# An attention and MLP backward kernel on one core: six late weight-gradient stores moved to the last two heads, the last MLP piece moved by four heads, and the first K load moved ahead of wq and wo

## The chip, the cores and the metric

The kernel runs on one core of a Trainium2 chip. Time is device microseconds of one execution. Three timed runs of the kernel before gave a median of 756.13 us (755.35 to 757.45). Smaller is better.

The core has a matrix engine (TensorE, PE), VectorE (DVE), ScalarE (ACT), GpSimd (POOL) and SyncE (SP). Each works through its own instructions in order. Sixteen DMA engines move data between device memory and the on-chip buffers. SP issues all large loads (queue q1 of the profile) and POOL issues all stores of gradients (queue q0).

## What is computed

One token is decoded through an attention block and a gated MLP in parallel, and the gradients of everything but one unused copy of x are taken back.

```python
xn  = layernorm(x)                       # 1 x 640
q   = xn @ wq                            # 32 heads of 128
p   = softmax(q . k_cache * 128**-0.5)   # per head, 8192 positions
o   = p . v_cache
h   = silu(xn @ w1) * (xn @ w3)          # 1728 wide
out = x + o @ wo + h @ w2
# returned: out, and the gradients for grad_out of
# x, k_cache, v_cache, wq, wo, w1, w3, w2
```

All arrays are bfloat16. k_cache and v_cache are 32 x 8192 x 128, 2 MB per head each. Their gradients are as large, and each is an outer product: dV of a head is p times do (the gradient of o), dK is ds times q. So the kernel reads some 152 MB and writes 151 MB, nearly all of it K, V, dK and dV.

## The kernel before

The loop goes over heads, with h from -1 to 31. An iteration finishes head h (called c in the code) and prepares head h + 1 (called n), and VectorE's order is the order in which the code is written. In one iteration VectorE does four products of a 2 MB tile half with a broadcast vector (`product`, line 270: two halves for the scores S of head n with K, two for DP with V), whose sums TensorE takes by multiplying with an identity (line 272), and four output tiles (`outer`, line 279: two halves of dV, two of dK of head c). Of a dV half, 24 of 32 position columns are made by VectorE and eight by ScalarE (line 283). Each output tile is one store of 1 MB, issued by POOL (line 285), from a pool of five buffers.

K and V have three buffers each. In iteration h the loads of V and K of head h + 3 are put into SP's queue (lines 113 and 107), each as soon as the code has used the buffer of head h. SP issues in order, so a load that waits for its buffer holds all later loads.

wq and wo are taken in groups of four heads (`load_group`, lines 119 to 125), two buffers each. Group g + 1 is loaded at the end of the iteration with h = 4g and prepared (`prep_steps`: q and do of four heads) in the following two. After the last head of a group, `finish_group` writes the gradients over the weights' own buffers and POOL stores them (line 238 for wo, line 242 for wq).

The MLP is cut into four pieces of 432 of its 1728 columns. A piece has one buffer `wt`, shared by all pieces, which holds w1, w3 and w2 of the piece (lines 146 to 150). The table `mlp_at` (line 462) says after which head a piece is loaded: 1, 9, 17 and 21 for pieces 0 to 3. Two heads later its steps are queued. `gap()` runs one step, four or five times a head, and steps of `prep_steps` and of the MLP wait in one list. A piece needs six steps, the first with VectorE's product at line 374, the last with the sum at line 452. So pieces 0 to 3 begin in heads 3, 11, 19 and 23 and end one head later. Its gradients are written over its weights and stored by POOL at line 431 and 433 (w2), and 446 (w1, then w3).

Before the loop, SP loads x, then wq and wo of group 0, then K and V of heads 0, 1 and 2 (lines 153 to 156). q of group 0 needs wq, do needs wo.

`row_dots` (line 321 to 325) takes the sum over DP times p. Its multiply writes a scratch tile `junk` that nothing reads. `E` holds a head's exponentials, and ScalarE reads it at line 311 for its share of dV.

After the loop, out and the gradient of x are formed from sums that were kept in `accbank` (lines 516 to 539).

The functions that the change touches, and the loop that calls them:

Of the kernel before, what the change touches and what calls it, by code (L numbers as in the profile page):

```python
# [10 lines left out]
F32 = mybir.dt.float32  # L11
ALU = mybir.AluOpType
ACTF = mybir.ActivationFunctionType
# [3 lines left out]
P = 128  # L17
# [4 lines left out]
def kernel(  # L22
# [22 lines left out]
    nc = tc.nc  # L45
    H = A_k_cache.shape[1]
    SK = A_k_cache.shape[2]
    DH = A_k_cache.shape[3]
# [4 lines left out]
    J = SK // P  # L53
    JH = J // 2
    RUN = 8
    GH = 4
    NG = H // GH
    ORDERED = {mybir.EngineType.DVE, mybir.EngineType.SP, mybir.EngineType.Pool}
    NPIECE = 4
    ACT_J = 8  # L60
    scale = float(DH) ** -0.5
# [8 lines left out]
    small = ctx.enter_context(tc.tile_pool(name="small", bufs=2))  # L70
# [7 lines left out]
    dkc = out_2.rearrange("b h (p j) d -> (b h) p j d", p=P)  # L78
    dvc = out_3.rearrange("b h (p j) d -> (b h) p j d", p=P)
    wq_v = A_wq.rearrange("(ci p) n -> p ci n", p=P)  # L80
    wo_v = A_wo.rearrange("(h p) c -> p h c", p=P)
    dwq_v = out_4.rearrange("(ci p) n -> p ci n", p=P)
    dwo_v = out_5.rearrange("(h p) c -> p h c", p=P)
# [5 lines left out]
    with tc.manual_schedule(engines=ORDERED):  # L89
# [15 lines left out]
        def load_k(h):  # L105
            Kt = kvpool.tile([P, J, DH], BF16, name="Kt", tag="K")
            nc.sync.dma_start(Kt[:], kc[h])
            kv_tiles[h] = kv_tiles.get(h, [None, None])
            kv_tiles[h][0] = Kt

        def load_v(h):
            Vt = kvpool.tile([P, J, DH], BF16, name="Vt", tag="V")
            nc.sync.dma_start(Vt[:], vc[h])
            kv_tiles[h] = kv_tiles.get(h, [None, None])
            kv_tiles[h][1] = Vt

        grp = {}

        def load_group(g):
            hs = slice(g * GH * DH, (g + 1) * GH * DH)  # L120
            wq_g = wload.tile([P, NC, GH * DH], BF16, name="wq_g", tag="wq_g")
            nc.sync.dma_start(wq_g[:], wq_v[:, :, hs])
            wo_g = wload.tile([P, GH, D], BF16, name="wo_g", tag="wo_g")
            nc.sync.dma_start(wo_g[:], wo_v[:, g * GH:(g + 1) * GH, :])
            grp[g] = dict(wq=wq_g, wo=wo_g)

        assert F % NPIECE == 0
        FP = F // NPIECE
# [9 lines left out]
        def load_piece(pc):  # L138
# [11 lines left out]
                nc.sync.dma_start(w2c[0:FP - NF * P, NF, :], B_w2[f0 + NF * P:f0 + FP, :])  # L150
            ml[pc] = (w1c, w3c, w2c)

        load_group(0)
        for h in range(min(3, H)):
            load_k(h)
            load_v(h)

# [77 lines left out]

        def finish_group(g):
            G_ = grp.pop(g)
            nc.gpsimd.dma_start(dwo_v[:, g * GH:(g + 1) * GH, :], G_["wo"][:])
            for ci in range(NC):
                nc.scalar.activation(G_["wq"][:, ci, :], G_["dqbc"][:].rearrange("p h d -> p (h d)"),  # L240
                                     ACTF.Copy, scale=xn_col[:, ci:ci + 1])
            nc.gpsimd.dma_start(dwq_v[:, :, g * GH * DH:(g + 1) * GH * DH], G_["wq"][:])


        hs = {}
# [26 lines left out]
                nc.tensor.matmul(ps[:], lhsT=ident_bf[:], rhs=T[:, :, RUN * i:RUN * (i + 1)],  # L272
                                 start=(half == 0 and i == 0), stop=(half == 1 and i == DHH // RUN - 1))

        def outer(st, vec, w2, dst, h, half, wf=None):
            j0 = half * JH
            JD = JH - (ACT_J if wf is not None else 0)
            ot = opool.tile([P, JH, DH // 2, 2], BF16, name="ot", tag="o")
            nc.vector.tensor_tensor(ot[:, 0:JD],  # L279
                                    vec.rearrange("p (a b) -> p a b", b=2).unsqueeze(1).to_broadcast([P, JD, DH // 2, 2]),  # L280
                                    w2[:, j0:j0 + JD, :].unsqueeze(2).to_broadcast([P, JD, DH // 2, 2]), ALU.mult)
            for j in range(JD, JH):
                nc.scalar.activation(ot[:, j].rearrange("p a b -> p (a b)"), vec, ACTF.Copy,  # L283
                                     scale=wf[:, half, j - JD:j - JD + 1])
            nc.gpsimd.dma_start(dst[h][:, j0:j0 + JH, :], ot[:].rearrange("p j a b -> p j (a b)"))  # L285
# [17 lines left out]
        def probs(st):  # L303
            rZ = small.tile([P, 1], F32, name="rZ")
            nc.vector.reciprocal(rZ[:], st.hb[:, 3:4])
            st.P2 = small.tile([P, J, 2], BF16, name="P2")
            nc.vector.tensor_scalar(st.P2[:], st.E[:].unsqueeze(2).to_broadcast([P, J, 2]), rZ[:], None, ALU.mult)
            st.Pf = None
            if ACT_J:
                st.Pf = small.tile([P, 2, ACT_J], F32, name="Pf")  # L310
                nc.scalar.activation(st.Pf[:], st.E[:].rearrange("p (a j) -> p a j", a=2)[:, :, JH - ACT_J:JH],
                                     ACTF.Copy, scale=rZ[:])

        def attend(st):
            for j in range(J):
# [3 lines left out]
        def row_dots(st):  # L319
            st.DP = small.tile([P, J], F32, name="DP_sb")  # L320
            nc.vector.tensor_reduce(st.DP[:], st.ps["DP"][:], AX.X, ALU.add)  # L321
            junk = small.tile([P, J], F32, name="junk", bufs=1)
            rdot = small.tile([P, 1], F32, name="rdot")
            nc.vector.scalar_tensor_tensor(junk[:], st.DP[:], 1.0, st.P2[:, :, 0], ALU.mult, ALU.mult, accum_out=rdot[:])
            nc.tensor.matmul(st.hb[:, 4:5], lhsT=ones_f[:], rhs=rdot[:], start=True, stop=True, skip_group_check=True)

        def dscores(st):
# [36 lines left out]
        def mlp_steps(pc):  # L364
# [63 lines left out]
                nc.scalar.copy(bc_sb[:, wi, :], bc_ps[:, 0:FP])  # L428
            for bi, (b0, rows) in enumerate(pblocks):
                nc.scalar.activation(w2c[0:rows, bi, :], g_bc_bf[0:rows, :], ACTF.Copy, scale=hcol[0:rows, bi:bi + 1])  # L430
            nc.gpsimd.dma_start(out_8[f0:f0 + NF * P, :].rearrange("(fb p) c -> p fb c", p=P), w2c[:, 0:NF, :])
            if NB > NF:
                nc.gpsimd.dma_start(out_8[f0 + NF * P:f0 + FP, :], w2c[0:FP - NF * P, NF, :])
            dx_ps = ps_w.tile([P, NC, DR1], F32, name="dx_ps", tag="w")
            for wi, (wt, dst) in enumerate(((w1c, dw1_v), (w3c, dw3_v))):
                yield
                T = tpool.tile([P, NC, FP], BF16, name="T13", tag="T")
                nc.vector.tensor_tensor(T[:], wt, bc_sb[:, wi, :].unsqueeze(1).to_broadcast([P, NC, FP]), ALU.mult)
                for i in range(FP // DR1):
                    nc.tensor.matmul(dx_ps[:], lhsT=ident_bf[:], rhs=T[:, :, DR1 * i:DR1 * (i + 1)],  # L440
                                     start=(wi == 0 and i == 0), stop=(wi == 1 and i == FP // DR1 - 1))
                nc.vector.tensor_tensor(wt.rearrange("p c (a b) -> p c a b", b=2),
                                        bc_sb[:, wi, :].rearrange("p (a b) -> p a b", b=2).unsqueeze(1)
                                        .to_broadcast([P, NC, FP // 2, 2]),
                                        xn2[:].unsqueeze(2).to_broadcast([P, NC, FP // 2, 2]), ALU.mult)
                nc.gpsimd.dma_start(dst[:, :, f0:f0 + FP], wt)
            yield
            if pc == 0:
                nc.vector.tensor_reduce(dxn_mlp[:], dx_ps[:], AX.X, ALU.add)
# [9 lines left out]
            if steps and next(steps[0], "end") == "end":  # L459
                steps.pop(0)  # L460

        mlp_at = {h0: pc for pc, h0 in enumerate((1, 9, 17, 21))}
        for _ in prep_steps(0):
            pass
        for h in range(-1, H):
            n = new_head(h + 1) if h + 1 < H else None
            c = hs.pop(h) if h >= 0 else None
            if h >= 0:
                g, hh = divmod(h, GH)
                if h - 2 in mlp_at:  # L470
                    steps.append(mlp_steps(mlp_at[h - 2]))
            if n:
                product(n, "S", 0)
            if c:
                probs(c)
                outer(c, c.do, c.P2, dvc, h, 0, c.Pf)
                gap()
                row_dots(c)
                attend(c)
            if n:  # L480
                product(n, "S", 1)
            if c:
                outer(c, c.do, c.P2, dvc, h, 1, c.Pf)
                if h + 3 < H:
                    load_v(h + 3)
                gap()
                dscores(c)
                outer(c, c.q, c.U2, dkc, h, 0)
            if n:
                row_max(n)  # L490
                product(n, "DP", 0)
            if c:
                outer(c, c.q, c.U2, dkc, h, 1)
                if h + 3 < H:
                    load_k(h + 3)
                gap()
            if n:
                exps(n)
                product(n, "DP", 1)
            if c:  # L500
                weights(c)
                gap()
                if hh == 0 and g + 1 < NG:
                    load_group(g + 1)
                if hh == 1 and g + 1 < NG:
                    steps.append(prep_steps(g + 1))
                    gap()
                if hh == 2 and g + 1 < NG:
                    gap()
                if h in mlp_at:  # L510
                    load_piece(mlp_at[h])
# [58 lines left out]
```

## Time and profile before

| What | Value |
|---|---|
| Median of three runs | 756.13 us |
| Profiled execution's own time | 755.72 us |
| Its span on the core | 753.9 us |
| TensorE clock granted, mean | 0.768 of full speed |
| Moved between memory and buffers | 304 MB, 403 GB/s over the span |
| Output stores | 128 of 1 MB, median 14.7 us from issue to landing |
| K loads, V loads | 32 each of 2 MB, median 16.7 and 14.2 us |
| wq and wo loads | 8 each of 640 KB, median 19.4 and 25.8 us |
| Loads of a piece: w1 and w3, w2 | 540 KB each, 480 + 60 KB; median 35.6, 33.3 and 15.6 us |

The profile is of one execution. Its rows of engines by time slice cut the span into 40 equal parts, and a digit is the busy share of a slice in tenths (9 is 90% or more). In a row of a group of instructions stand the line, engine, operation and tiles, then how many, busy time, mean duration, and the engine's idle time in front of them with what ended most of it. In a row of the timeline stand the start and the duration in us, and in brackets how long the engine sat idle in front of it and what it waited for. In a table of stretches stand the stretch, its length, then the busy time and number of instructions of TensorE, its weight loads, VectorE, ScalarE and GpSimd, then TensorE's clock, the DMA share and GB/s. SPq and POOLq are the sequencers that issue DMAs.

### The profile page before, as it was taken

The page shows a single profiled execution, that of the slowest core. Times are in us where ns is not written, and L with a number is a line of the kernel's source. Part 1 is how long each engine was busy: PE and PEld are TensorE (multiplying, and loading weights), DVE is VectorE, ACT ScalarE, POOL GpSimd, SP SyncE. Part 2 cuts the span into 40 slices and gives each one's busy share as a digit, 9 for nine tenths or more (in the row PEclk, how much of TensorE's full clock was granted, in tenths as well). Part 3 has the DMA queues.
Part 4 walks back from the last instruction along what each step waited for, and adds up shares of the span by engine and source line. Part 5 has one row for each costly group of instructions (what it writes and reads, how often), then busy time and mean ns, then how long its engine had stood idle before and what let it go on. Part 6 is the DMA issues. An engine that isn't in the chain of part 4 may idle for free.

```text
span 753.9 us, 15362 instructions
## 1 busy us (share of the span) xinstructions
PE 555.0 (74%) x6451; PEld 325.0 (43%) x6451; DVE 669.8 (89%) x732; ACT 310.1 (41%) x866; POOL 97.9 (13%) x172
## 2 busy tenths in 40 slices
PE   3787677878776678786877667867868788777672
PEld 2354344445443445443544344434534545434342
DVE  4899879999997679999999868899969999999894
ACT  4334417235443542533435144343542534443244
POOL 0011012011110101200011100121101211011011
PEclk9869967579976785878979687587966677987675
DMA  8999999999999999999999999999999999999857
GB/s 324 425 425 420 415 418 407 388 421 429 426 424 421 421 417 419 362 398 427 426 425 419 420 419 420 409 348 417 427 411 428 369 406 428 429 424 425 372 224 293
DMA packets 50201, 304.00 MB, mean 403 GB/s; under 512 B 5460, under 2 KB 21780, under 8 KB 25556
## 3 DMA queue, kind: packets, MB, share of 16 engines
q1 hardware_dynamic: 26612, 151.51, 49.1%
q0 software_dynamic: 22720, 151.35, 48.9%
q8 instruction: 50, 0.82, 0.4%
q10 hardware_dynamic: 800, 0.17, 0.1%
q14 instruction: 19, 0.16, 0.1%
HBM read 151.67 MB, written 151.34 MB: 402 GB/s over the span
## 4 chain that ended last, share of the span: by engine, by line
DVE 37%; DMA 35%; SPq 11%; PE 8%; issue 7%; POOL 1%; POOLq 0%; DVEq 0%
DMA out_dram<-ot 18%; DVE T L270 16%; DVE ot L279 12%; DMA wt<-in_B_w_dram 11%; SPq L148 6%; DMA wo_g<-in_A_wo_dram 4%; SPq L147 3%; PE psS L272 2%; PE psDP L272 2%; DMA Kt<-in_A_k_cache_dram 2%; DVE DP_sb L321 1%; DVE S_sb L289 1%; PE hb L332 1%; PE dh_ps L377 1%; PE hb L316 1%
## 5 line engine op out<-in xcount | busy, mean ns | idle before, releaser
L272 PE MATMUL psDP<-T,ident_bf 128*128 128x512 bf16 x512 | 187.7, 531 | 76.1 <-DVE T L270 76.1
L272 PEld LDWEIGHTS <-ident_bf 128*128 128x128 bf16 x1024 | 121.4, 121 | 233.6 <-issue 181.6
L283 ACT ACTIVATE ot<-do_g,Pf 128x128 bf16<-128x128 bf16 x512 | 155.7, 392 | 14.2 <-DMA out_dram<-ot 13.7
L270 DVE TENSOR_TENSOR T<-Kt,qs_g 128x4096 bf16<-128x4096 bf16 x64 | 146.4, 2289 | 9.5 <-PE psDP L272 6.3
L272 PE MATMUL psS<-T,ident_bf 128*128 128x512 bf16 x512 | 150.6, 444 | 5.6 <-DVE T L270 5.4
L279 DVE TENSOR_TENSOR ot<-qs_g,U 128x4096 bf16<-128x4096 bf16 x64 | 146.4, 2288 | 4.3 <-DMA out_dram<-ot 3.4
L270 DVE TENSOR_TENSOR T<-Vt,do_g 128x4096 bf16<-128x4096 bf16 x64 | 146.0, 2281 | 0.0
L285 POOL DMA_DIRECT2D out_dram<-ot x128 | 68.8, 538 | 577.6 <-ACT ot L283 278.3
L279 DVE TENSOR_TENSOR ot<-do_g,P 128x3072 bf16<-128x3072 bf16 x64 | 112.3, 1755 | 10.0 <-DMA out_dram<-ot 8.8
L300 ACT ACTIVATE E<-S_sb,negM 128x64 f32<-128x64 f32 x32 | 11.1, 347 | 190.9 <-DVE negM L297 190.9
L332 PEld LDWEIGHTS <-Kt 128*128 128x128 bf16 x2048 | 58.5, 99 | 21.5 <-issue 18.7
L332 PE MATMUL hb<-U,Kt 128*128 128x1 bf16 x2048 | 57.5, 164 | 7.4 <-DVE U L329 7.1
L316 PEld LDWEIGHTS <-Vt 128*128 128x128 bf16 x2048 | 57.4, 99 | 0.0
L316 PE MATMUL hb<-P,Vt 128*128 128x1 bf16 x2048 | 56.4, 163 | 0.0
L346 ACT ACTIVATE wo_g<-g_bc_bf,odq 128x640 bf16<-128x640 bf16 x32 | 26.5, 827 | 70.2 <-PE accbank L344 70.1
L292 PE MATMUL hb<-ident_f,mrow 128*128 128x128 f32 x64 | 17.7, 365 | 26.4 <-DVE mrow L291 26.4
L356 ACT ACTIVATE dq_diag<-ident_bf,odq 128x128 bf16<-128x128 bf16 x32 | 12.9, 402 | 52.8 <-DVE odq L340 52.8
L351 ACT COPY wqT<-ps_wqT 128x640 bf16<-128x640 bf16 x32 | 21.7, 680 | 15.3 <-PE ps_wqT L349 15.3
L225 ACT COPY woT<-ps_t 128x512 bf16<-128x512 bf16 x40 | 22.3, 581 | 13.4 <-PE ps_t L223 13.4
L430 ACT ACTIVATE wt<-g_bc_bf,hcol 128x640 bf16<-128x640 bf16 (+1 forms) x16 | 12.4, 821 | 36.9 <-DVE t L410 18.7
L223 PE MATMUL ps_t<-ident_bf,wo_g 128*128 128x128 bf16 x160 | 17.8, 244 | 10.6 <-DMA wo_g<-in_A_wo_dram 10.5
L301 PEld LDWEIGHTS hb<-rsum,ones_f 128*128 128x128 f32 x64 | 16.3, 271 | 21.1 <-ACT E L300 19.3
(122 smaller groups left out, 479.7 us busy)
## 6 DMA issues: line engine op xcount, KB each, us to landing
out_dram<-ot POOLq DMA_DIRECT2D x128, 1024.0 KB, 14.7
Kt<-in_A_k_cache_dram SPq DMA_DIRECT2D x32, 2048.0 KB, 16.7
Vt<-in_A_v_cache_dram SPq DMA_DIRECT2D x32, 2048.0 KB, 14.2
wq_g<-in_A_wq_dram SPq DMA_DIRECT2D x8, 640.0 KB, 19.4
wo_g<-in_A_wo_dram SPq DMA_DIRECT2D x8, 640.0 KB, 25.8
out_dram<-wo_g POOLq DMA_DIRECT2D x8, 640.0 KB, 7.3
out_dram<-wq_g POOLq DMA_DIRECT2D x8, 640.0 KB, 5.9
wt<-in_B_w_dram SPq DMA_DIRECT2D x8, 540.0 KB, 35.6
```

Of the source, the lines that this page charges most:

```text
L147: nc.sync.dma_start(w1c, w1_v[:, :, f0:f0 + FP])
L148: nc.sync.dma_start(w3c, w3_v[:, :, f0:f0 + FP])
L225: nc.scalar.copy(woT[:], ps_t[:])
L270: nc.vector.tensor_tensor(T[:], src[:, :, ds_], vec[:, ds_].unsqueeze(1).to_broadcast([P, J, DHH]), ALU.mult)
L272: nc.tensor.matmul(ps[:], lhsT=ident_bf[:], rhs=T[:, :, RUN * i:RUN * (i + 1)], start=(half == 0 and i == 0), stop=(half == 1 and i == DHH ...
L279: nc.vector.tensor_tensor(ot[:, 0:JD], vec.rearrange("p (a b) -> p a b", b=2).unsqueeze(1).to_broadcast([P, JD, DH // 2, 2]), w2[:, j0:j0 ...
L283: nc.scalar.activation(ot[:, j].rearrange("p a b -> p (a b)"), vec, ACTF.Copy, scale=wf[:, half, j - JD:j - JD + 1])
L285: nc.gpsimd.dma_start(dst[h][:, j0:j0 + JH, :], ot[:].rearrange("p j a b -> p j (a b)"))
L316: nc.tensor.matmul(st.hb[:, 0:1], lhsT=st.V[:, j, :], rhs=st.P2[:, j, 0:1], start=(j == 0), stop=(j == J - 1), skip_group_check=True)
L332: nc.tensor.matmul(st.hb[:, 1:2], lhsT=st.K[:, j, :], rhs=st.U2[:, j, 0:1], start=(j == 0), stop=(j == J - 1), skip_group_check=True)
L346: nc.scalar.activation(G_["wo"][:, hh, :], g_bc_bf[:], ACTF.Copy, scale=odq[:, 0:1])
L351: nc.scalar.copy(wqT[:], ps_wqT[:])
```

## The change

Three things change in what the kernel issues, and one in what it writes.

- The start table has 25 in place of 21 for the last MLP piece: its loads follow those of head 28, its steps run in heads 27 and 28.
- Six stores are collected in a list and issued at the top of the iteration with h = 30, ahead of everything else in it: the four of the last MLP piece (w2 in two parts, w1, w3) and the two of the next to last weight group (wo and wq of group 6). All other stores stay where they are.
- K of head 0 is loaded ahead of wq and wo of group 0, V of head 0 behind them.
- `row_dots` writes its scratch result over `E` of the same head in place of `junk`.

The rest of the difference moves an argument of `outer` to another place and drops a condition that is always true.

```diff
         grp = {}
+        late = []
+
+        def store(dst, src, later=False):
+            if later:
+                late.append((dst, src))
+            else:
+                nc.gpsimd.dma_start(dst, src)
...
+        load_k(0)
         load_group(0)
-        for h in range(min(3, H)):
+        load_v(0)
+        for h in range(1, min(3, H)):
             load_k(h)
             load_v(h)
...
         def finish_group(g):
             G_ = grp.pop(g)
-            nc.gpsimd.dma_start(dwo_v[:, g * GH:(g + 1) * GH, :], G_["wo"][:])
+            store(dwo_v[:, g * GH:(g + 1) * GH, :], G_["wo"][:], g == NG - 2)
...
-            nc.gpsimd.dma_start(dwq_v[:, :, g * GH * DH:(g + 1) * GH * DH], G_["wq"][:])
+            store(dwq_v[:, :, g * GH * DH:(g + 1) * GH * DH], G_["wq"][:], g == NG - 2)
...
-            junk = small.tile([P, J], F32, name="junk", bufs=1)
             rdot = small.tile([P, 1], F32, name="rdot")
-            nc.vector.scalar_tensor_tensor(junk[:], st.DP[:], 1.0, st.P2[:, :, 0], ALU.mult, ALU.mult, accum_out=rdot[:])
+            nc.vector.scalar_tensor_tensor(st.E[:], st.DP[:], 1.0, st.P2[:, :, 0], ALU.mult, ALU.mult, accum_out=rdot[:])
...
-            nc.gpsimd.dma_start(out_8[f0:f0 + NF * P, :].rearrange("(fb p) c -> p fb c", p=P), w2c[:, 0:NF, :])
+            last_pc = pc == NPIECE - 1
+            store(out_8[f0:f0 + NF * P, :].rearrange("(fb p) c -> p fb c", p=P), w2c[:, 0:NF, :], last_pc)
             if NB > NF:
-                nc.gpsimd.dma_start(out_8[f0 + NF * P:f0 + FP, :], w2c[0:FP - NF * P, NF, :])
+                store(out_8[f0 + NF * P:f0 + FP, :], w2c[0:FP - NF * P, NF, :], last_pc)
...
-                nc.gpsimd.dma_start(dst[:, :, f0:f0 + FP], wt)
+                store(dst[:, :, f0:f0 + FP], wt, last_pc)
...
-        mlp_at = {h0: pc for pc, h0 in enumerate((1, 9, 17, 21))}
+        mlp_at = {h0: pc for pc, h0 in enumerate((1, 9, 17, 25))}
...
                 if h - 2 in mlp_at:
                     steps.append(mlp_steps(mlp_at[h - 2]))
+            if h == H - 2:
+                for dst, src in late:
+                    store(dst, src)
             if n:
                 product(n, "S", 0)
```

More of the change, by code (lines that the diff above doesn't have):

```diff
@@ L273, in product, with outer @@
                                  start=(half == 0 and i == 0), stop=(half == 1 and i == DHH // RUN - 1))
-        def outer(st, vec, w2, dst, h, half, wf=None):
+        def outer(st, vec, w2, wf, dst, h, half):
             j0 = half * JH
@@ L307, in probs @@
             nc.vector.tensor_scalar(st.P2[:], st.E[:].unsqueeze(2).to_broadcast([P, J, 2]), rZ[:], None, ALU.mult)
[L308 to L312, printed above, removed]
+            st.Pf = small.tile([P, 2, ACT_J], F32, name="Pf")
+            nc.scalar.activation(st.Pf[:], st.E[:].rearrange("p (a j) -> p a j", a=2)[:, :, JH - ACT_J:JH],
+                                 ACTF.Copy, scale=rZ[:])
         def attend(st):
@@ L475 @@
                 probs(c)
-                outer(c, c.do, c.P2, dvc, h, 0, c.Pf)
+                outer(c, c.do, c.P2, c.Pf, dvc, h, 0)
                 gap()
@@ L482 @@
             if c:
-                outer(c, c.do, c.P2, dvc, h, 1, c.Pf)
+                outer(c, c.do, c.P2, c.Pf, dvc, h, 1)
                 if h + 3 < H:
@@ L487 @@
                 dscores(c)
-                outer(c, c.q, c.U2, dkc, h, 0)
+                outer(c, c.q, c.U2, None, dkc, h, 0)
             if n:
@@ L492 @@
             if c:
-                outer(c, c.q, c.U2, dkc, h, 1)
+                outer(c, c.q, c.U2, None, dkc, h, 1)
                 if h + 3 < H:
```

## The prediction

> **What bounds the kernel now.** I read the page's busy shares and slices, then the queues, then VectorE's waits, then a table of stretches cut at the four places where VectorE takes up an MLP piece (line 374), and last VectorE's timeline there and at the end.
>
> ```profile
> PE 555.0 (74%) x6451; PEld 325.0 (43%) x6451; DVE 669.8 (89%) x732; ACT 310.1 (41%) x866; POOL 97.9 (13%) x172
> DVE  4899879999997679999999868899969999999894
> DMA  8999999999999999999999999999999999999857
> q1 hardware_dynamic: 26612, 151.51, 49.1%
> q0 software_dynamic: 22720, 151.35, 48.9%
> ```
>
> Two resources are nearly full: VectorE at 89%, and the DMA engines, whose two queues take 98% of the span between them and whose row is 9 until three slices from the end. So a gain must come out of transfer time that ends late, and only as long as VectorE is not last.
>
> ```profile
> 98.00:281.00 183.00, 138.50 (x1613) 81.37 (x1613) 165.52 (x176) 74.95 (x211) 24.17 (x41) 0.76 1.01 418
> 281.00:465.00 184.00, 137.48 (x1619) 81.09 (x1617) 166.01 (x177) 76.37 (x216) 23.84 (x41) 0.78 1.01 413
> 465.00:562.00 97.00, 75.20 (x858) 43.85 (x856) 87.84 (x101) 41.74 (x118) 14.28 (x24) 0.75 1.00 402
> 562.00:699.00 137.00, 107.83 (x1261) 63.05 (x1259) 129.59 (x142) 55.69 (x155) 19.25 (x32) 0.76 1.01 416
> 712.00:734.00 22.00, 17.30 (x206) 10.15 (x205) 21.58 (x23) 9.53 (x31) 2.14 (x4) 0.77 0.57 232
> 734.00:754.00 20.00, 5.41 (x146) 4.62 (x144) 9.43 (x21) 9.14 (x22) 3.76 (x6) 0.60 0.71 276
> ```
>
> The third pair of numbers is VectorE's busy time, the last two are the DMA share and GB/s. Up to 562 the DMA share is 1.00 and VectorE idles 9 to 18 us in each stretch. From 562 on VectorE idles little (7.4 of 137 us), and from 712 to 734 it is full while DMA is at 0.57.
>
> ```profile
> DVE T L374 <- DMA wt<-in_B_w_dram: 18.7, 4, 6.0
> DVE U L329 <- PE hb L316: 13.6, 5, 5.5
> DVE ot L279 <- DMA out_dram<-ot: 12.3, 10, 3.1
> ```
>
> VectorE's idle time in the loop is waiting for weights (directly, and through TensorE's in-order queue at line 316) and for a free output buffer.
>
> ```profile
> 97.78 1.49 DVE L374 TENSOR_TENSOR T<-wt,g_bc_bf 128x2560 bf16<-128x2560 bf16 x1 [5.85 <-DMA wt<-in_B_w_dram]
> 280.87 1.49 DVE L374 TENSOR_TENSOR T<-wt,g_bc_bf 128x2560 bf16<-128x2560 bf16 x1 [3.64 <-DMA wt<-in_B_w_dram]
> 464.73 1.49 DVE L374 TENSOR_TENSOR T<-wt,g_bc_bf 128x2560 bf16<-128x2560 bf16 x1 [3.17 <-DMA wt<-in_B_w_dram]
> 553.91 1.76 DVE L279 TENSOR_TENSOR ot<-do_g,P 128x3072 bf16<-128x3072 bf16 x1
> 561.69 1.49 DVE L374 TENSOR_TENSOR T<-wt,g_bc_bf 128x2560 bf16<-128x2560 bf16 x1 [6.02 <-DMA wt<-in_B_w_dram]
> 699.42 1.76 DVE L279 TENSOR_TENSOR ot<-do_g,P 128x3072 bf16<-128x3072 bf16 x1 [3.10 <-DMA out_dram<-ot]
> 714.84 1.76 DVE L279 TENSOR_TENSOR ot<-do_g,P 128x3072 bf16<-128x3072 bf16 x1
> 732.35 1.76 DVE L279 TENSOR_TENSOR ot<-do_g,P 128x3072 bf16<-128x3072 bf16 x1
> ```
>
> These rows carry the sum. Pieces 0 to 3 begin at 97.78, 280.87, 464.73 and 561.69 (heads 3, 11, 19, 23), each after a wait for its weights. The last row is the first dV product of head 31; it ends at 734.11, and 19.8 us later the span ends.
>
> That the stretches are transfer-bound can be worked out. From the trace's packets, spread over 16 engines: a K or V load takes 4.99 us, an output store 2.50, a group's wq and wo 3.7 in and 3.4 out, a piece's weights 4.8 in and 5.1 out. Eight heads with two groups and a piece: 16 x 4.99 + 32 x 2.50 + 2 x 7.1 + 9.9 = 183.9, against 183.1 and 183.9 measured between pieces. Four heads with one group and a piece: 96.9, against 97.0. A piece thus begins when the transfers ahead of it are done.
>
> **The change, part by part.**
> *Piece 3 moves by four heads* (the start heads go from 21 to 25). Its loads go behind K of head 28 in SP's queue, its steps from heads 23 and 24 to 27 and 28. The stretch from piece 2 to piece 3 becomes heads 19 to 27 with groups at 20 and 24: the same transfers as in the two eight-head stretches. I take their mean, 183.5: piece 3 starts at 464.7 + 183.5 = 648.2. In the trace of before the same place in head 27 is passed at 652.4; it arrives 4 us earlier, but with the piece's VectorE work still to do.
>
> What comes after it: after piece 2 VectorE ran from 464.73 to 555.67, four heads and the piece in 90.9 us, 1.4 of it idle, though transfers were at 1.00. The same work follows piece 3 now, less the S product that head 31 has no successor for (732.35 - 714.84 = 17.5 against a usual 19.75: 2.2). So the first dV product of head 31 ends at 648.2 + 90.9 - 2.2 = 736.9, against 734.1: **+2.8 us**. As a check by idle time from 464.73 to there: before, 1.4 + 6.0 + 1.3 + 4.7 (four waits for output buffers at 657 to 702) = 13.4. After, an eight-head stretch has 15.2 (1.2 + 2.0 + 3.3 + 5.5 + 3.2) and the rest 1.4: 16.6, or +3.2.
>
> *Stores held back.* Six stores leave the queue of POOL in heads 27 and 28 (w2 in two parts, wo, wq, w1, w3; 5.1 + 3.4 = 8.5 us of engine time) and stand in front of head 30's. Nothing waits for their buffers: no later piece or group takes them. They free transfer time between 648 and 715, where the forecast has VectorE as the bound already: worth 0. The cover is VectorE's 90.9 us. Without it, at most the 4.7 us of output-buffer waits were to be had, and I have counted those as gone. Above, those waits could stay, +4.7. I take none, by the nearest row: the stretch after piece 2 had none with its stores in place.
>
> In POOL's queue they cost 0.78 + 0.53 + 0.78 + 0.88 + 0.87 + 0.87 = 4.7 us, between head 29's last issue (709.8) and head 30's first (718.4): a gap of 8.1, so it fits. Their data runs from about 713 + 3. From 715 to 741 the store queue was busy 14.0 of 26 us, so 12 are free for 8.5: 0, and at most 8.5 if all of it came ahead of the last stores. The end of the kernel (last four output stores, wo and wq of group 7, DMA share 0.71) stays 19.8 us.
>
> *K of head 0 first.* In the trace wq landed at 8.1, wo at 9.9, K at 14.8, and the first product began at 14.9. Now K takes the front (5.0 us), wq lands about 12.5, and TensorE's five products with the copy (10.73 to 13.68: 2.95) end about 15.5: VectorE starts 0.6 later. Bounds: wq right behind K at 11.6 gives -0.3, wq as last of the three at 14.8 gives +2.9. V of head 0 keeps its place. wo, needed for the V product at 22.2, is 5.1 us from do_g and comes at about 20. Price 0 either way: VectorE waits 5.85 at piece 0, more than any of these, and the DMA engines never run dry (1.02 from 5 to 98). Without that cover, +0.6.
>
> *The scratch of row_dots becomes E.* VectorE's multiply now waits until ScalarE has read E (line 311). That reading ended before the multiply in all 32 heads, by 0.27 us or more. Cost 0; half a microsecond of delay in the nine tightest heads would be some 2 us, inside the transfer-bound stretches.
>
> Sum: +2.8 on a span of 753.9, 756.7. The profiled execution took 755.72 (1.8 outside the span), 0.4 under the median of 756.13; the forecast for the median is 758.9.
>
> One rule speaks against the held-back run of issues. The Trainium skill (SBUF — State Buffer, "SBUF: two separate sides") says that VectorE in its two-port mode locks GpSimd out of the SBUF port that it writes DMA descriptors through, so that such DMAs look blocked. Here it would make each of six issues wait for an operation of 2.28 us; this trace doesn't show it: POOL issued at 590.27 and 591.14, 0.88 and 0.87 us each, beside VectorE's products.
>
> **The rivals.**
> *Weights in time* (faster). If piece 3 didn't have to wait, 5.5 + 3.2 of the 15.2 idle would go: piece 3 at 639.5, 5.9 under before, 750.2. For it: SP has nothing else to fetch between groups. Against: all four pieces waited, and the transfers add up to the stretch. It decides where piece 3 starts before 645.4. Chance 0.12, with all 8.5 us coming off the end (747.6) in it.
> *Half of that* (no change). Only the wait at line 374 goes: 2.8 - 3.2, 755.7. Chance 0.12.
> *Output buffers still late* (slower). The waits of 4.7 us return in heads 28 to 30, because loads of four more tiles and stores compete until about 700: 763.6. Chance 0.08.
> *A stretched run of issues* (slower). POOL held at each issue: 6 x 2.28 = 13.7 in place of 4.7, so head 30's first store is issued at 727 and its buffer, which head 31 wants at 737.8, is free at about 740: some 3 us more, 762. Chance 0.02. The end of 8.5 us (all the held-back data ahead of the last stores, 767) has less than 0.01 and stays outside the range.
>
> **How the numbers follow.** The forecast holds 0.66, from 757 to 760.5 (mostly the 183.1 to 183.9 of the stretch and +-1 in its place). About 0.3% (2.3 us) is what a measurement of this kernel can tell from no change; 0.72 of the forecast's chance lies above that. Slower: 0.66 x 0.72 + 0.10 = 0.58. Same: 0.18 + 0.12 = 0.30. Faster: 0.12. The range reaches down to half the wait gone, 755.0, and up into the output-buffer case, 762.5.
>
> **What would show it.** Piece 3's line-374 product near 648 after a wait for weights of 3 us or more; a DMA share of 1.00 until about 700; VectorE with under 2 us idle from there to head 31; six issues at about 713 to 718 and a DMA share near 0.9 from 715 to 725; an unchanged 19.8 us at the end; the first product at about 15.5. I am wrong if piece 3 starts before 645, if the wait there is gone, or if waits for output buffers stay in heads 28 to 30.

## The result and the profile after

The changed kernel takes 760.01 us (median of six runs, 758.98 to 761.36), the kernel before 756.01 (six runs, 755.35 to 757.45). The ratio is 1.0046, 95% interval 1.0031 to 1.0062: slower by 0.46%, some 3.5 us (the two medians lie 4.0 apart, the profiled spans 3.3). Forecast were 758.9 us and +2.8. The profiled execution took 758.98 us, with a span of 757.2; the one of before took 755.72 with 753.9.

First from the page of the changed kernel: span, busy shares, VectorE's and the DMA engines' row, and the queues.

```profile
span 757.2 us, 15393 instructions
PE 553.9 (73%) x6451; PEld 326.9 (43%) x6451; DVE 670.0 (88%) x732; ACT 310.3 (41%) x866; POOL 97.9 (13%) x172
DVE  4899889999998679999999878899999796889994
DMA  8999999999999999999999999999999999969887
q1 hardware_dynamic: 26612, 151.51, 48.9%
q0 software_dynamic: 22720, 151.35, 48.8%
```

VectorE's busy time is what it was (670.0 against 669.8 us), and so are the transfers. The 3.3 us of span are idle time of both. In the DMA row a 6 stands five slices from the end, where before there were 9s; the 5 of before, in the last slice but one, is now an 8. The hole in the transfers has been filled at the end and opened anew in front of it.

VectorE's timeline of the changed kernel at the places that were shown of before (line 381 is 374 of before, 289 is 279, 280 is 270, 282 is 272, 324 is 316, 336 is 329):

```profile
97.70 1.49 DVE L381 TENSOR_TENSOR T<-wt,g_bc_bf 128x2560 bf16<-128x2560 bf16 x1 [5.09 <-DMA wt<-in_B_w_dram]
281.00 1.49 DVE L381 TENSOR_TENSOR T<-wt,g_bc_bf 128x2560 bf16<-128x2560 bf16 x1 [3.69 <-DMA wt<-in_B_w_dram]
464.76 1.49 DVE L381 TENSOR_TENSOR T<-wt,g_bc_bf 128x2560 bf16<-128x2560 bf16 x1 [3.26 <-DMA wt<-in_B_w_dram]
648.41 1.49 DVE L381 TENSOR_TENSOR T<-wt,g_bc_bf 128x2560 bf16<-128x2560 bf16 x1 [2.96 <-DMA wt<-in_B_w_dram]
672.56 2.29 DVE L280 TENSOR_TENSOR T<-Kt,qs_g 128x4096 bf16<-128x4096 bf16 x1 [1.41 <-PE psDP L282]
735.81 1.76 DVE L289 TENSOR_TENSOR ot<-do_g,P 128x3072 bf16<-128x3072 bf16 x1
740.60 0.35 DVE L336 SCALAR_TENSOR_TENSOR U<-DP_sb,hb,P 128x128 bf16<-128x128 f32 x1 [0.41 <-PE hb L324]
```

Up to piece 2 the two executions run alike (464.73 and 464.76). Piece 3 starts 183.65 us behind piece 2, as piece 2 did behind piece 1, and after a wait for its weights. From there to the U product at 740.60, the last row, the 1.41 at 672.56 is VectorE's only wait over 0.3 us. The four waits for output buffers at 657 to 702 of before are gone. The first dV product of head 31 (735.81) ends at 737.57, 3.5 us later than before, and the span ends 19.6 us behind it.

Stretches of the changed kernel:

```profile
649.00:664.00 15.00, 13.12 (x158) 8.13 (x159) 14.59 (x21) 0.94 (x4) 1.60 (x3) 0.51 1.00 421
664.00:683.00 19.00, 14.18 (x154) 9.01 (x152) 17.03 (x27) 14.72 (x35) 0.53 (x1) 0.68 0.64 271
683.00:699.00 16.00, 12.74 (x114) 6.58 (x113) 15.72 (x17) 2.54 (x8) 1.60 (x3) 0.77 1.00 378
699.00:713.00 14.00, 10.42 (x150) 6.20 (x149) 13.82 (x14) 4.89 (x18) 1.68 (x4) 0.68 0.84 347
713.00:726.00 13.00, 10.44 (x135) 6.41 (x134) 12.68 (x14) 7.15 (x23) 6.28 (x9) 0.89 0.93 320
```

Between 664 and 683, inside the piece's steps, the DMA engines are at 0.64: POOL issued no output store from 663.85 to 680.27, and the load of V of head 31 was issued only at 682.96, when the buffer of head 28 came free. With the piece moved and nothing held back (the first experiment) output stores and loads pause in the same way, but there the six stores run in that stretch and the share is 0.95. So the pause comes from the compute engines (VectorE begins no output tile between 660.74 and 675.36, and ScalarE begins its share of the next one at 677.53), and the hole is the place that the held stores left. Here transfers wait for the computing. At 713 to 726 the share is 0.93, where the six held stores run.

### The profile page after: what moved, and what is told of

The parts are those of the page before. It is cut to its first block, busy times and chain, and to the rows that moved or that the text cites. A ratio compares the mean times of both kernels' runs of the same rounds, so it can differ in the third digit from the quotient of the medians.

```text
span 757.2 us, 15393 instructions
## 1 busy us (share of the span) xinstructions
PE 553.9 (73%) x6451; PEld 326.9 (43%) x6451; DVE 670.0 (88%) x732; ACT 310.3 (41%) x866; POOL 97.9 (13%) x172
## 4 chain that ended last, share of the span: by engine, by line
DVE 47%; DMA 27%; SPq 10%; issue 8%; PE 5%; ACT 1%; POOL 1%; POOLq 0%; DVEq 0%; ACTq 0%
DVE T L280 20%; DVE ot L289 17%; DMA out_dram<-ot 15%; DMA wt<-in_B_w_dram 11%; SPq L156 5%; SPq L155 3%; PE psDP L282 2%; DVE DP_sb L329 2%; DMA wq_g<-in_A_wq_dram 1%; SPq L154 1%; DVE S_sb L299 1%; PE hb L339 1%; DVE U L336 1%; DVE T L381 1%; DVE E L331 1%
## 5 line engine op out<-in xcount | busy, mean ns | idle before, releaser
L282 PE MATMUL psDP<-T,ident_bf 128*128 128x512 bf16 x512 | 183.3, 521 | 73.3 <-DVE T L280 73.3
L336 DVE SCALAR_TENSOR_TENSOR U<-DP_sb,hb,P 128x128 bf16<-128x128 f32 x32 | 11.2, 350 | 16.9 <-PE hb L324 16.9
```

## The experiments

Each ratio is to runs of the kernel before that stand in the same record: 21 with a median of 757.41 us for the first four experiments, 23 with 757.23 for the others. The profiled execution of before took 755.72, so a difference of profiled spans and a ratio need not agree to the last 2 us.

### Each half of the change alone

The kernel before with nothing but the piece moved:

```diff
-        mlp_at = {h0: pc for pc, h0 in enumerate((1, 9, 17, 21))}
+        mlp_at = {h0: pc for pc, h0 in enumerate((1, 9, 17, 25))}
```

> The kernel before with nothing but the last MLP piece moved (start head 25 in place of 21); no store held back. Theory (VectorE's work of piece 3 comes behind a start that the transfers fix): piece 3's line-374 product at 648 to 649, 90 us of VectorE work behind it with under 2 us of waits, span 756 to 757.5, so 2 to 3.5 us slower than before, like the changed kernel. Rival 1 (the six held stores cost it, by their issues on POOL and by their data ahead of the last stores): within 1 us of before. Rival 2 (holding saves part of what moving costs): the waits for output buffers in heads 28 to 30, 4.7 us, are back, and this is 3 to 5 us slower than the changed kernel.

Measured: ratio to before 1.0049 (1.0036 to 1.0063), profiled span 757.6. VectorE's timeline of this run at piece 3 and at head 31, and three of its stretches:

```profile
647.68 1.49 DVE L374 TENSOR_TENSOR T<-wt,g_bc_bf 128x2560 bf16<-128x2560 bf16 x1 [1.86 <-DMA wt<-in_B_w_dram]
671.38 2.29 DVE L270 TENSOR_TENSOR T<-Kt,qs_g 128x4096 bf16<-128x4096 bf16 x1 [1.11 <-PE psDP L272]
737.08 0.69 DVE L321 TENSOR_REDUCE DP_sb<-psDP 128x64 f32<-128x512 f32 x1 [1.13 <-PE psDP L272]
```

```profile
648.00:699.00 51.00, 40.02 (x433) 23.65 (x430) 48.81 (x63) 21.75 (x59) 9.05 (x14) 0.70 0.99 398
664.00:683.00 19.00, 13.85 (x135) 8.51 (x136) 17.54 (x20) 14.12 (x35) 5.26 (x7) 0.74 0.95 384
715.00:737.00 22.00, 17.76 (x193) 9.69 (x192) 20.53 (x22) 9.09 (x29) 2.14 (x4) 0.73 0.48 194
```

The move alone costs all that the change costs. There is no wait for an output buffer behind piece 3, though the six stores run at their old places in 648 to 699 (DMA share 0.99). So within the intervals, some 1 us, the held stores cost nothing in the changed kernel (rival 1 falls) and bring nothing there either (rival 2 falls).

Then the kernel before with nothing but the stores held back, as in the change, and piece 3 left at 21:

```diff
+            if h == H - 2:
+                for dst, src in late:
+                    store(dst, src)
...
-                nc.gpsimd.dma_start(dst[:, :, f0:f0 + FP], wt)
+                store(dst[:, :, f0:f0 + FP], wt, last_pc)
```

> The kernel before with nothing but the six stores held back to the top of head 30 (piece 3 stays at start head 21). Theory: up to piece 3's product at 561.7 nothing changes; 8.5 us of transfers leave a stretch that is transfer-bound, and the 4.7 us for which VectorE waits for output buffers at 657 to 702 go, so 3 to 5 us faster than before, with the end at 19.8 us behind the first dV product of head 31 as before. Rival 1 (held stores cost): 2 to 4 us slower than before. Rival 3 (transfers hidden anyway): within 1 us.

Measured: ratio 0.9938 (0.9925 to 0.9951), some 4.7 us faster, profiled span 751.2. VectorE's timeline (line 380 is 374 of before, 278 is 270, 335 is 329) holds every wait over 0.3 us from 500 to the end of the heads but one of 0.98 at 731, behind TensorE's DP sums; then two stretches:

```profile
562.50 1.49 DVE L380 TENSOR_TENSOR T<-wt,g_bc_bf 128x2560 bf16<-128x2560 bf16 x1 [5.91 <-DMA wt<-in_B_w_dram]
586.65 2.29 DVE L278 TENSOR_TENSOR T<-Kt,qs_g 128x4096 bf16<-128x4096 bf16 x1 [1.40 <-PE psDP L280]
734.32 0.35 DVE L335 SCALAR_TENSOR_TENSOR U<-DP_sb,hb,P 128x128 bf16<-128x128 f32 x1 [0.41 <-PE hb L322]
```

```profile
562.00:699.00 137.00, 110.04 (x1287) 65.21 (x1288) 132.73 (x145) 58.10 (x163) 15.00 (x27) 0.72 0.99 411
712.00:731.00 19.00, 13.69 (x160) 7.69 (x159) 18.02 (x19) 7.10 (x25) 2.19 (x4) 0.73 0.91 347
```

The waits for output buffers of before, 4.7 us in all, were these three and the one of 3.10 at 699.42:

```profile
657.98 2.29 DVE L279 TENSOR_TENSOR ot<-qs_g,U 128x4096 bf16<-128x4096 bf16 x1 [0.51 <-DMA out_dram<-ot]
678.56 2.29 DVE L279 TENSOR_TENSOR ot<-qs_g,U 128x4096 bf16<-128x4096 bf16 x1 [0.60 <-DMA out_dram<-ot]
701.92 2.29 DVE L279 TENSOR_TENSOR ot<-qs_g,U 128x4096 bf16<-128x4096 bf16 x1 [0.47 <-DMA out_dram<-ot]
```

They are gone, and VectorE does 132.7 us of work from 562 to 699 where it did 129.6. From 712 on the transfers are at 0.91 where they were at 0.57. The profiled spans differ by less than the ratio says, 2.7 us: piece 3 starts 0.8 later in this execution than in that of before, and the wait of 0.98 at 731 has no counterpart there. The same six stores, held in the same way, are thus worth 4.7 us with piece 3 at 21 and nothing with piece 3 at 25: hold and move together give +0.46%, the move alone +0.49%. The version that only holds is faster than both kernels.

### The two small parts alone

K of head 0 first:

```diff
+        load_k(0)
         load_group(0)
-        for h in range(min(3, H)):
+        load_v(0)
+        for h in range(1, min(3, H)):
```

> The kernel before with nothing but K of head 0 ahead of wq and wo. Theory: the first product starts 0.5 to 1.2 us later (15.4 to 16.1), the wait for weights at piece 0 is shorter by as much, piece 0 starts at 97.8 within 0.3, and the time is within 1 us of before. Rival (the later start is carried to the end): 1 to 1.5 us slower.

The scratch result over E:

```diff
-            junk = small.tile([P, J], F32, name="junk", bufs=1)
...
-            nc.vector.scalar_tensor_tensor(junk[:], st.DP[:], 1.0, st.P2[:, :, 0], ALU.mult, ALU.mult, accum_out=rdot[:])
+            nc.vector.scalar_tensor_tensor(st.E[:], st.DP[:], 1.0, st.P2[:, :, 0], ALU.mult, ALU.mult, accum_out=rdot[:])
```

> The kernel before with nothing but the scratch result of row_dots written over E. Theory: the gap ahead of the multiply grows by some 0.08 us a head, 2.5 us in all, of which only what lies behind piece 3 (8 heads, 0.6 us) can show: 0 to 1 us slower. Rival: the whole 2.5 us shows, or ScalarE's reading holds VectorE for longer in the nine tight heads: 2 to 4 us slower.

Measured: 0.9998 (0.9986 to 1.0011) for K first, 1.0001 (0.9989 to 1.0012) for the scratch. VectorE's timeline with K first:

```profile
16.04 4.49 DVE L272 TENSOR_TENSOR T<-Kt,qs_g 128x4096 bf16<-128x4096 bf16 x2 [3.90 <-ACT qs_g L218]
97.92 1.49 DVE L376 TENSOR_TENSOR T<-wt,g_bc_bf 128x2560 bf16<-128x2560 bf16 x1 [4.96 <-DMA wt<-in_B_w_dram]
```

The first product now waits for q (it waited for K) and starts at 16.04 in place of 14.90. At piece 0 the wait is 4.96 in place of 5.85, and the piece starts at 97.92 in place of 97.78: the later start is lost in the first wait for weights.

### What VectorE's work of piece 3 costs in either place

From both kernels a part of piece 3's VectorE work is left out, its loads and stores kept (what is missing stands in the expectation):

```diff
-                T = tpool.tile([P, NC, FP], BF16, name="T13", tag="T")
-                nc.vector.tensor_tensor(T[:], wt, bc_sb[:, wi, :].unsqueeze(1).to_broadcast([P, NC, FP]), ALU.mult)
...
+                if pc < NPIECE - 1:
+                    T = tpool.tile([P, NC, FP], BF16, name="T13", tag="T")
+                    nc.vector.tensor_tensor(T[:], wt, bc_sb[:, wi, :].unsqueeze(1).to_broadcast([P, NC, FP]), ALU.mult)
...
```

> The changed kernel with part of piece 3's VectorE work left out: both products for the gradient of x (with their TensorE sums) and both products that make the gradients of w1 and w3, so the stores of piece 3 carry the weights themselves and the gradient of x lacks piece 3. Loads and stores stay. 4 x 1.28 + 0.6 = 5.7 us of VectorE go, and the wait of 1.4 behind the TensorE sums. Theory (VectorE is the bound from piece 3's start at 648 on): 5.5 to 7 us faster than the changed kernel, span 750 to 752. Rival (the end is set by transfers or by the held stores): under 3 us faster.

> The kernel before with the same part of piece 3's VectorE work left out (5.7 us, and 1.3 of waiting). Theory: here piece 3 stands in heads 23 and 24, and the transfers are the bound up to some 700, so most of it comes back as waits for output buffers: 0 to 3.5 us faster than before, with those waits grown from 4.7 us. Rival (VectorE's work costs the same wherever it stands): 5.5 to 7 us faster than before.

Measured: from the changed kernel, ratio to before 0.9948 (0.993 to 0.9965), profiled span 751.7 against 757.2 with the work, 5.5 us and as expected; the ratios, 0.9948 against 1.0046, put it at 7.4 us, and either is far above the rival's 3. Piece 3 starts at 647.98 (648.41 with the work). From the kernel before, 0.9996 (0.9985 to 1.0006), span 754.4: no gain. VectorE's timeline of that last run shows where the work went, all waits over 0.3 us from piece 3 to head 31:

```profile
561.99 1.49 DVE L374 TENSOR_TENSOR T<-wt,g_bc_bf 128x2560 bf16<-128x2560 bf16 x1 [4.06 <-DMA wt<-in_B_w_dram]
611.26 1.76 DVE L279 TENSOR_TENSOR ot<-do_g,P 128x3072 bf16<-128x3072 bf16 x1 [1.95 <-DMA out_dram<-ot]
616.10 2.29 DVE L279 TENSOR_TENSOR ot<-qs_g,U 128x4096 bf16<-128x4096 bf16 x1 [2.82 <-DMA out_dram<-ot]
638.15 0.35 DVE L329 SCALAR_TENSOR_TENSOR U<-DP_sb,hb,P 128x128 bf16<-128x128 f32 x1 [2.62 <-PE hb L316]
678.37 2.29 DVE L279 TENSOR_TENSOR ot<-qs_g,U 128x4096 bf16<-128x4096 bf16 x1 [0.38 <-DMA out_dram<-ot]
699.35 1.76 DVE L279 TENSOR_TENSOR ot<-do_g,P 128x3072 bf16<-128x3072 bf16 x1 [3.22 <-DMA out_dram<-ot]
701.85 2.29 DVE L279 TENSOR_TENSOR ot<-qs_g,U 128x4096 bf16<-128x4096 bf16 x1 [0.48 <-DMA out_dram<-ot]
737.37 0.36 DVE L329 SCALAR_TENSOR_TENSOR U<-DP_sb,hb,P 128x128 bf16<-128x128 f32 x1 [0.41 <-PE hb L316]
```

Behind its start the waits from 611 to 702 add up to 11.5 us where they were 4.7: 6.8 of the 7.0 us taken out (5.7 of work, 1.3 of waiting) came back. In heads 23 and 24 this work is covered by transfers; in heads 27 and 28 it stands in the path at full price. That is the cause of the loss, and it is shown from both sides: the same work taken out is worth 5.5 to 7.4 us behind the move and nothing ahead of it.

### Pieces still earlier

If covered work costs nothing, pieces still earlier might leave all 8.5 us of held transfers to be gained. Both with and without holding, the table was

```diff
-        mlp_at = {h0: pc for pc, h0 in enumerate((1, 9, 17, 21))}
+        mlp_at = {h0: pc for pc, h0 in enumerate((1, 5, 9, 13))}
```

> The kernel before with the six stores held back to the top of head 30 and the pieces loaded after heads 1, 5, 9 and 13, so that no MLP work stands in the last 15 heads. Theory: a longer transfer-bound stretch lies ahead of the end and all 8.5 us of held transfers can come out of it, against 4.7 us with piece 3 at 21: 5 to 8.5 us faster than before, at most 3.5 us faster than the version that only holds. Rival (the waits for weights just come closer together and cost VectorE more): slower than the version that only holds.

> The kernel before with the pieces loaded after heads 1, 5, 9 and 13 and nothing held back. Theory: the same transfers end at the same time, so within 1.5 us of before, and the waits for output buffers in heads 16 to 30 are longer by what piece 3's wait in head 23 was. Rival (an earlier last piece is what helps, not the holding): 3 us faster or more.

Measured: 0.9958 (0.9943 to 0.9974) with holding, 1.0021 (1.001 to 1.0031) without. The expectation of 5 to 8.5 us failed: 3.2 us, and not better than holding with piece 3 at 21 (0.9938). Whether it is worse, as the rival had it, stays open, since the intervals overlap. Without holding, the 1.6 us of loss are just outside the 1.5 that were expected. VectorE's timeline with holding, its last waits before the end of the heads, then the last stretches:

```profile
610.07 1.76 DVE L287 TENSOR_TENSOR ot<-do_g,P 128x3072 bf16<-128x3072 bf16 x1 [2.27 <-DMA out_dram<-ot]
612.67 2.29 DVE L287 TENSOR_TENSOR ot<-qs_g,U 128x4096 bf16<-128x4096 bf16 x1 [0.58 <-DMA out_dram<-ot]
637.60 0.36 DVE L335 SCALAR_TENSOR_TENSOR U<-DP_sb,hb,P 128x128 bf16<-128x128 f32 x1 [5.50 <-PE hb L322]
```

```profile
699.00:715.00 16.00, 12.36 (x110) 6.59 (x111) 15.76 (x17) 4.93 (x16) 5.78 (x8) 0.68 0.97 366
715.00:731.00 16.00, 11.75 (x106) 6.02 (x104) 14.62 (x16) 5.11 (x19) 2.19 (x4) 0.69 0.84 332
731.00:751.00 20.00, 5.80 (x150) 4.94 (x148) 9.19 (x20) 9.21 (x22) 3.76 (x6) 0.59 0.71 276
```

From 637.60 to 730 VectorE has no wait over 0.3 us, so its work from there on sets the end, and transfers freed behind that point buy nothing. The wait at 637.60 belongs to the weights of the last group: TensorE waits for them until 631.03, and what VectorE needs stands behind that in its queue. All versions need these weights there, but with piece 3 at 21 VectorE does not wait for them (no wait over 0.3 us from 586.65 to 731 in the version that only holds). Against the version without holding that wait ends 2.4 us earlier (637.60 against 640.02), and 2.9 us of waits at 700 (2.47 and 0.47) are gone. Why the early table costs 0.2% by itself was not followed up.

## Why the prediction was right

**Piece 3's start.** Forecast 648.2 after a wait of 3 us or more; it is 648.41 after 2.96. The step behind it, that a piece starts when the transfers ahead of it are done, held: three stretches of eight heads took 183.3, 183.8 and 183.65 us. The faster rival, weights in time, did not come: piece 3 would have had to start before 645.4.

**VectorE's work behind it.** Forecast 88.7 us to the end of head 31's first dV product; it took 89.2 (737.57 - 648.41). Half a microsecond was not in the sum. The gap before the multiply of `row_dots` grew from 0.04 to some 0.11 us a head, 0.3 in the four heads of this stretch, and two short operations beside POOL's run of issues took 0.4 us longer together (below). The first had been priced at 0, the second was not in the forecast; together they are a little more than the half microsecond. The gap grows in the same way in the run with nothing but the scratch result over `E`. In the changed kernel ScalarE had read `E` 0.49 us or more before the multiply in every head, so VectorE did not stand waiting for that reading; why the gap is longer all the same is not shown.

**Stores held back.** Priced at 0, with 4.7 us of output-buffer waits counted as gone. Both held: the waits are gone, and with the piece at 25 they go without the holding too. What was wrong is the cover named for the transfers, a DMA share of 1.00 until about 700. It is 0.64 from 664 to 683, where it is 0.95 with the stores left in place: while VectorE and ScalarE work on the piece, output buffers are not filled and K and V buffers do not come free, so nothing takes the place of the stores that were held back. That follows from the prediction's own terms: transfers that are freed while VectorE is the bound leave a hole. The price stays 0. The slower rival, output buffers still late, fell with it.

**POOL's issues.** Forecast 4.7 us at 713 to 718. From POOL's timeline:

```profile
713.45 1.31 POOL L124 DMA_DIRECT2D out_dram<-wt  x2
714.75 0.80 POOL L124 DMA_DIRECT2D out_dram<-wo_g  x1
715.54 0.88 POOL L124 DMA_DIRECT2D out_dram<-wq_g  x1
717.28 1.73 POOL L124 DMA_DIRECT2D out_dram<-wt  x2 [0.86 <-issue]
721.51 0.59 POOL L295 DMA_DIRECT2D out_dram<-ot  x1 [2.50 <-ACT ot L293]
```

That is 4.72 us of issuing and a gap of 0.86, done at 719.0, and head 30's first output store follows when ScalarE has finished its part. The stretched run of issues, 13.7 us, was not seen. The lock on descriptor writing that the Trainium skill describes (SBUF — State Buffer, "SBUF: two separate sides") is one of VectorE's two-port mode. The rival took it to hold for products of 2.28 us with two inputs, and no run here shows that these run in that mode; so the trace goes against the rival and not against the lock.

**K first.** The first product was forecast at 15.5 and came at 15.87, 1.0 later than before in place of 0.6. wq let TensorE start at 12.91, and its five products with the copy took the 2.95 that were assumed. Price 0 held, in the run with that part alone too.

**The end.** 19.8 us forecast, 19.6 measured. **The sum:** 756.7 forecast for the span, 757.2 measured; the errors of its parts, +0.2 at the start, +0.5 behind it and -0.2 at the end, are too small for the sum to have come out right by chance. The rest of the distance between 758.9 and 760.01 is the spread from run to run: the changed kernel's profiled run is 1.0 under its median, that of before was 0.4 under the one I started from.

## What to carry to other kernels

Before stores are held back or work is moved, find the last point at which the critical engine still waits for a transfer. In this kernel, compute ahead of it was free and bytes cost; behind it, bytes were free and compute cost. A change that moves both in the same direction can lose with one what it gains with the other: here holding six stores was worth 4.7 us by itself, and moving the MLP piece cost 3.7 (0.49%) and left the stores nothing to gain. Before, VectorE's last waits for transfers, at 657 to 702, came behind the piece's work; with the piece moved the last one is that for its own weights, at 648.41, and the work comes behind it. Further ahead is not better by itself: with the pieces at 1, 5, 9 and 13 the last such wait went to 637.60, and holding was worth 3.2 us.

## What the runs showed that was not expected

Beside POOL's run of issues short VectorE operations take longer, and the issues do not. In the changed kernel the cast of odq took 0.41 us at 715.13 beside it (0.17 elsewhere) and the product for P 0.49 at 717.69 (0.28). In the version that only holds, the cast took 0.53 and the product for P 0.40. All four kernels that hold the stores have at least one such operation there; in the other six no cast of odq is over 0.2 us and no product for P over 0.32. The 2.28 us products were not longer.

In six of the eight experiments (not in the two main profiles) VectorE waits 1.0 to 1.1 us for the DP sums of head 31. There TensorE's last eight of these took 3.57 us, with a granted clock of 0.51 from 732 to 738 (piece moved alone); in the changed kernel they took 1.89, with 0.78 in the same stretch. From TensorE's timeline, first with the piece moved alone, then the changed kernel:

```profile
733.48 3.57 PE L272 MATMUL psDP<-T,ident_bf 128*128 128x512 bf16 x8 [0.81 <-DVE T L270]
```

```profile
735.10 1.89 PE L282 MATMUL psDP<-T,ident_bf 128*128 128x512 bf16 x8 [0.81 <-DVE T L280]
```

So about 1 us of the time goes with the clock that TensorE is granted in the last head. The profiled executions of the two kernels both lack this wait, so it is no part of the 3.3 us between them; but it is in the spans of six of the experiments, and it is as much as a third of what the change costs.
